# Attention: which engine forms the last half of each second head's low part

## The chip, the cores and the metric

The kernel is one program for one core of one Trainium2 chip. A core has engines that run side by side, each through its own instructions in their fixed order: TensorE (PE in the profile, its weight loads PEld), VectorE (DVE), ScalarE (ACT), GpSimd (POOL), and SyncE (SP), which here only starts DMA transfers. An instruction waits at the head of its engine's queue until what it needs is there, and all behind it on that engine wait with it. The metric is the time of one execution on the device in microseconds (us), the median of several runs. 1 us is 1000 ns.

## The reference, cut to what matters

Two layers, each an attention A and a gated MLP B, with a residual around each. The change lies in A, in the part where the softmax weights `p` meet the values.

```python
for s in range(N):                         # 4 segments of 512 rows, 32 heads of 20 columns
    qs, ks, vs = q[:, :, s], k[:, :, s], v[:, :, s]
    logits = jnp.einsum("bhqd,bhkd->bhqk", qs, ks) * scale + mask
    p = _softmax(logits, axis=-1)
    a_dot = jnp.einsum("bhqk,bhkd->bhqd", p, vs)
...
x = x + _A_ref(_layernorm(x, axis=-1), A_wq, A_wk, A_wv, A_wo, A_beta)
x = x + _B_ref(_layernorm(x, axis=-1), B_w_in, B_w_sp, B_b_sp, B_w_out)
x = x + _A_ref(_layernorm(x, axis=-1), A_wq, A_wk, A_wv, A_wo, A_beta)
x = x + _B_ref(_layernorm(x, axis=-1), B_w_in, B_w_sp, B_b_sp, B_w_out)
```

The products run on fp16 operands. So that little precision is lost, each fp32 operand is split in two fp16 parts: the high part is its rounding, the low part is what the rounding left over. For the softmax weights these are `PH` (high) and `PL = P - PH` (low), and both are multiplied with the values.

## The kernel before, in words

A layer's attention (`phase1a`) treats the 32 heads two at a time, in each of the four segments: 64 pairs of heads per layer, numbered `n`. Time is cut into steps `t` in `run`; five steps are a round, and a round carries two pairs, 2d and 2d+1, through the same stations. The order of the PE's instructions is that of the code (`manual_schedule` for PE alone); on the other engines a scheduler fixes the order when the program is built, within the limits that `issue_after` sets: `behind(DVE)` puts what is traced inside it behind the row maxima of the same step, `behind(ACT)` behind the exponentials of the same step.

In each step PE does, in this order: the logits by queries (`by_queries`, tile `mp` in PSUM, one buffer), from which DVE takes the row maxima (L935 and L938, `mxs`); the logits by keys (`by_keys`, tile `es`, one buffer), from which ACT forms the exponentials `P` (L913); the products of `PH` and `PL` with the values for the heads whose turn it is (`pvs`, L977, into `pv`); and then a share of the dense products (L677, L709, L736), which are spread over the steps. Since `mp` has one buffer, PE's logits of the next step wait for the row maxima of this one. DVE also finishes each pair (`combine`: `rs`, its reciprocal, `ab`, lines L988, L989, L993), splits the dense products, and does the layernorm statistics.

`cast` makes the two parts of a pair's head `h`: ACT copies `P` to `PH` (L947, 1280 columns), and then two instructions of 640 columns each form `PL` (L949). Before the change both run on GpSimd, but for head 1 of the layer's last two pairs (`TAIL`), where they run on DVE. In a round the heads are cast at steps 2, 3, 4 and 5 (that is step 0 of the next round): (2d, head 0), (2d, head 1), (2d+1, head 0), (2d+1, head 1). PE uses them at steps 5, 6, 8 and 8. `PL` has two buffers, so the low part of one head can be formed only after PE has read that of the head two before it. GpSimd also adds the two halves of each finished pair (L996, L997) and splits the finished heads (L1006).

Of the kernel before, what the change touches and what calls it, by code (L numbers as in the profile page):

```python
# [14 lines left out]
ALU = mybir.AluOpType  # L15
# [555 lines left out]
DVE, ACT = mybir.EngineType.DVE, mybir.EngineType.Activation  # L571


class Attention:
# [366 lines left out]
    def cast(self, n, h):  # L941

        nc = self.nc
        P = self.pair(n)
        PH = self.pl3.tile([128, 1280], F16, tag="PH", name="PH")
        PL = self.pl2.tile([128, 1280], F16, tag="PL", name="PL")
        nc.scalar.copy(PH, P[:, h])  # L947
        for c in (slice(0, 640), slice(640, 1280))[::-1 if n % 2 and h else 1]:
            (nc.gpsimd if h == 0 or n < self.N - self.TAIL else nc.vector).tensor_tensor(PL[:, c], P[:, h, c], PH[:, c], ALU.subtract)  # L949
        self.P[n, h] = (PH, PL)  # L950

    def maxes(self, d):
# [287 lines left out]
```

## Time and profile before

| | |
|---|---|
| median of 3 runs | 2309.6 us (2309.24 to 2312.05) |
| span of the profiled execution | 2318.3 us |
| first layer's rounds (from the first to the last L935) | 80.6 us to about 570 us |
| second layer's rounds | 1227 us to 1698 us |
| the remainder | the MLP of each layer, PE busy all along |

The profile's span is that of one execution, 8.7 us above the median of the runs; the runs themselves differ by 3 us. In the page, a row of the busy table gives an engine's busy time, its share of the span and its number of instructions. A row of the view by stretches gives the same per stretch of the span: the stretch, its length, then busy time and count of each engine. A row of the view of waits gives engine, line and tile that waited, for whom, the sum, how many times, and the longest. A row of the timeline gives start, duration, engine, line, operation, shapes and count; in brackets, the idle time of the engine ahead of it.

### The profile page before, as it was taken

What the parts mean: (1) busy time and instruction counts of PE and PEld (TensorE: products, weight loads), DVE (VectorE), ACT (ScalarE), POOL (GpSimd) and SP (SyncE); (2) the same over time, 40 slices, a digit from 0 to 9 for tenths busy, and PEclk for the clock granted to TensorE, in tenths of its full rate; (3) what the DMA queues carried; (4) which work ended last, traced back from release to release, by engine and by line L of the source; (5) the groups of instructions that cost most, each with busy time, mean ns of one, the idle gap of its engine ahead of it and who ended that gap; (6) DMA issues with size and microseconds to landing.
All of it is one profiled execution on the core that took longest, in us unless ns stands there. A gap on an engine that the chain in (4) does not pass through costs nothing.

```text
span 2318.3 us, 52548 instructions
## 1 busy us (share of the span) xinstructions
PE 2174.6 (94%) x21706; PEld 1309.5 (56%) x21706; DVE 1377.8 (59%) x2577; ACT 1139.2 (49%) x1344; POOL 991.4 (43%) x976
## 2 busy tenths in 40 slices
PE   5888898999899999999998989999989999999998
PEld 3455555666555555555555556566665555555554
DVE  7687888777755444444427786777766444534331
ACT  3587788888522222121125987888863222212110
POOL 2287889999611000000104988899991100000000
PEclk9999999999899999999999999999999999999999
DMA  5565665345743687565633465443565357766561
GB/s 166 145 164 150 168 172 132 89 113 142 207 119 96 153 219 168 149 168 148 147 96 97 111 157 129 120 109 107 128 177 124 99 119 202 158 160 160 157 147 46
DMA packets 504912, 325.59 MB, mean 140 GB/s; under 512 B 410688, under 2 KB 445632, under 8 KB 499552
## 3 DMA queue, kind: packets, MB, share of 16 engines
q1 hardware_dynamic: 504672, 322.23, 54.5%
q8 instruction: 170, 2.79, 0.5%
q14 instruction: 70, 0.57, 0.1%
HBM read 148.46 MB, written 85.61 MB: 101 GB/s over the span
## 4 chain that ended last, share of the span: by engine, by line
PE 66%; DVE 9%; DMA 8%; POOL 6%; ACT 6%; issue 3%; SPq 1%; DVEq 0%; ACTq 0%; POOLq 0%
PE gp L430 23%; PE zp L343 13%; PE cyp L459 8%; POOL PL L949 5%; PE pv L977 3%; PE qps L736 3%; PE kps L736 3%; PE vps L677 3%; PE mp L875 3%; DVE mxs L938 2%; PE yps L709 2%; PE es L875 2%; ACT P L913 1%; ACT PH L947 1%; DMA th<-xnhl 1%
## 5 line engine op out<-in xcount | busy, mean ns | idle before, releaser
L949 POOL TENSOR_TENSOR PL<-P,PH 128x640 f16<-128x640 f32 x380 | 538.8, 1444 | 53.2 <-PE pv L977 45.6
L430 PE MATMUL gp<-zh,wt 128*128 128x432 f16 x2048 | 462.2, 346 | 0.0
L430 PEld LDWEIGHTS <-wt 128*128 128x128 f16 x3072 | 300.5, 98 | 257.6
L938 DVE TENSOR_REDUCE mxs<-mp 128x2 f32<-128x1024 f32 (+2 forms) x384 | 320.4, 862 | 148.1 <-PE mp L866 146.5
L913 ACT ACTIVATE P<-es,sc 128x1024 f32<-128x1024 f32 (+1 forms) x256 | 271.6, 1061 | 100.0 <-PE es L866 89.5
L445 POOL MEMSET un<- 128x64 f16 x32 | 4.9, 152 | 665.3 <-DMA ut<-un 628.3
L343 PEld LDWEIGHTS <-th 128*128 128x128 f16 x1920 | 187.3, 98 | 169.4 <-DMA th<-xnhl 8.8
L430 PE MATMUL gp<-zl,wt 128*128 128x432 f16 x1024 | 270.5, 346 | 0.0
L433 ACT ACTIVATE u<-gp,bsp,un 128x864 f32<-128x864 f32 x32 | 34.3, 1071 | 431.2 <-PE gp L430 431.2
L252 POOL TENSOR_TENSOR lnrs<-lnve,mhalf 128x1 f32<-128x1 f32 x96 | 60.8, 641 | 429.1 <-DVE lnve L251 377.5
L947 ACT CAST PH<-P 128x1280 f16<-128x1280 f32 x192 | 239.7, 1248 | 1.5
L407 DVE TENSOR_REDUCE am<-wr 128x1 f32<-128x2048 f32 x32 | 73.2, 2286 | 220.0 <-DMA wr<-in_B_w_sp_dram 220.0
L677 PE MATMUL vps<-wvh,xt 128*128 128x320 f16 x640 | 158.5, 316 | 25.6 <-DVE relu L768 19.4
L949 POOL TENSOR_TENSOR PL<-Pb,PH 128x640 f16<-128x640 f32 x124 | 178.0, 1462 | 9.2 <-PE pv L977 9.2
L459 PE MATMUL cyp<-wuh,ut 128*128 128x320 f16 (+1 forms) x896 | 165.1, 301 | 5.7 <-DMA ut<-un 5.7
L875 PEld LDWEIGHTS <-qk 64*128 64x128 f16 (+1 forms) x2048 | 78.0, 94 | 163.0 <-issue 140.3
L459 PEld LDWEIGHTS <-ut 128*128 128x128 f16 (+1 forms) x1344 | 132.1, 98 | 61.5 <-DMA ut<-un 6.4
L977 PE MATMUL pv<-vs,PL 128*128 128x41 f16 x2560 | 157.6, 181 | 8.4 <-POOL PL L949 6.9
L977 PE MATMUL pv<-vs,PH 128*128 128x41 f16 x2560 | 160.0, 182 | 1.2 <-DVE ab L993 1.2
L875 PE MATMUL es<-qk 64*128 64x512 f16 (+3 forms) x1024 | 126.3, 303 | 31.7 <-ACT P L913 27.1
L343 PE MATMUL zp<-wi1h,th 128*128 128x432 f16 x640 | 147.8, 346 | 6.8 <-DMA th<-xnhl 6.8
L343 PE MATMUL zp<-wi0h,th 128*128 128x432 f16 x640 | 148.1, 346 | 0.0
(189 smaller groups left out, 4315.8 us busy)
## 6 DMA issues: line engine op xcount, KB each, us to landing
wr<-in_B_w_sp_dram SPq DMA_DIRECT2D x32, 1024.0 KB
qk<-st SPq DMA_DIRECT2D x256, 120.0 KB
z<-z SPq DMA_DIRECT2D x32, 432.0 KB
cz<-z SPq DMA_DIRECT2D x32, 432.0 KB
xt<-in_A_x_dram SPq DMA_DIRECT2D x32, 320.0 KB
st<-qhl SPq DMA_DIRECT2D x40, 256.0 KB
st<-khl SPq DMA_DIRECT2D x40, 256.0 KB
x<-x SPq DMA_DIRECT2D x32, 320.0 KB
```

The costliest lines, as they stand in the source:

```text
L343: nc.tensor.matmul(zp[:, n, :FHH], a[:, k, :], b[:, k, c:c + FHH], start=(k == 0 and j == 0), stop=(k == KD - 1 and j == 2))
L407: nc.vector.tensor_reduce(am, wr, AX.X, ALU.max, apply_absolute_value=True)
L430: nc.tensor.matmul(gp[:, n, :FHH], wt[:, k // 8, a, k % 8, :], b[:, k, n * FHH:(n + 1) * FHH], start=(k == 0 and j == 0), stop=(k == NT - ...
L459: nc.tensor.matmul(yp[:, n, :320], a[:kn[k], k, :], b[:kn[k], k, n * 320:(n + 1) * 320], start=(k == 0 and j == 0), stop=(k == KO - 1 and ...
L677: nc.tensor.matmul(ps, a[:, k, c], b[:, k, n * 320:(n + 1) * 320], start=(i == 0), stop=(i == 14))
L736: nc.tensor.matmul(ps, a[:, k, c], b[:, k, :], start=(i == 0), stop=(i == 14))
L875: nc.tensor.matmul(out[:, h, o:o + w], a[r, ac], b[r, bc], start=o == 0, stop=False, skip_group_check=True)
L913: self.lead.append(nc.scalar.activation(P, E, AF.Exp, scale=g.esc))
L938: e = nc.vector.tensor_reduce(mx[:, :, n, j], mp[:, :, o:o + w], AX.X, ALU.max)
L947: nc.scalar.copy(PH, P[:, h])
L949: (nc.gpsimd if h == 0 or n < self.N - self.TAIL else nc.vector).tensor_tensor(PL[:, c], P[:, h, c], PH[:, c], ALU.subtract)
L977: nc.tensor.matmul(pv[:, i, h, :], x[:, c:c + 128], v[:, j, h0 + h, :], start=(j == 0 and x is PH), stop=(j == i and x is PL), skip_group_ ...
```

## The change

The halves of head 1's low part are told apart: the second of the two goes to DVE in all pairs, not only the last two, and what goes to DVE is put behind the row maxima of its step. The first half of head 1, and both halves of head 0, stay on GpSimd. In the layer's last two pairs both halves of head 1 stay on DVE, now also behind the row maxima.

```diff
-        for c in (slice(0, 640), slice(640, 1280))[::-1 if n % 2 and h else 1]:
-            (nc.gpsimd if h == 0 or n < self.N - self.TAIL else nc.vector).tensor_tensor(PL[:, c], P[:, h, c], PH[:, c], ALU.subtract)
+        for i, c in enumerate((slice(0, 640), slice(640, 1280))[::-1 if n % 2 and h else 1]):
+            if h and (i or n >= self.N - self.TAIL):
+                with self.behind(DVE):
+                    nc.vector.tensor_tensor(PL[:, c], P[:, h, c], PH[:, c], ALU.subtract)
+            else:
+                nc.gpsimd.tensor_tensor(PL[:, c], P[:, h, c], PH[:, c], ALU.subtract)
```

62 instructions of each layer move, 124 in all: GpSimd keeps 380 of its 504 on this line, DVE has 132 in place of 8. The line numbers behind it grow by four (L949 becomes L951 on DVE and L953 on GpSimd, L988 becomes L992, and so on). PE's instructions stand as before, in every row. On ACT, SP and DVE the scheduler also exchanges some neighbours.

First place: DVE in the first layer's round at 493 us to 498 us of the profile of before, behind the two row maxima of the round's step 1 (the row with x2) up to the next maxima. Before:

```order
L938 TENSOR_REDUCE mxs_289<-mp 128x2 x2
L715 SCALAR_TENSOR_TENSOR xt<-yps,sc,xt 128x320
L988 TENSOR_TENSOR rs<-pv,iomg 128x8
L989 RECIPROCAL rs<-rs 128x8
L993 TENSOR_TENSOR ab<-pv,rs 128x328
L938 TENSOR_REDUCE mxs_288<-mp 128x2
```

and now:

```order
L938 TENSOR_REDUCE mxs_289<-mp 128x2 x2
L715 SCALAR_TENSOR_TENSOR xt<-yps,sc,xt 128x320
L951 TENSOR_TENSOR PL<-Pb,PH 128x640
L992 TENSOR_TENSOR rs<-pv,iomg 128x8
L993 RECIPROCAL rs<-rs 128x8
L997 TENSOR_TENSOR ab<-pv,rs 128x328
L938 TENSOR_REDUCE mxs_288<-mp 128x2
```

The half low part of pair 2d+1 now stands ahead of a finished pair's three instructions and of the next row maxima.

Second place: DVE a little later in the same round, behind the two row maxima of step 3 up to the four maxima of step 4 (L935). Before:

```order
L938 TENSOR_REDUCE mxs_288<-mp 128x2 x2
L715 SCALAR_TENSOR_TENSOR xt<-yps,sc,xt 128x320
L988 TENSOR_TENSOR rs<-pv,iomg 128x8
L989 RECIPROCAL rs<-rs 128x8
L993 TENSOR_TENSOR ab<-pv,rs 128x328
L935 TENSOR_REDUCE mxs_288<-mp 128x2x2
```

and now:

```order
L938 TENSOR_REDUCE mxs_288<-mp 128x2 x2
L715 SCALAR_TENSOR_TENSOR xt<-yps,sc,xt 128x320
L992 TENSOR_TENSOR rs<-pv,iomg 128x8
L993 RECIPROCAL rs<-rs 128x8
L997 TENSOR_TENSOR ab<-pv,rs 128x328
L951 TENSOR_TENSOR PL<-P,PH 128x640
L935 TENSOR_REDUCE mxs_288<-mp 128x2x2
```

The half low part of pair 2d, head 1, stands directly ahead of L935. In some rounds it stands directly behind it.

Third place: GpSimd in that round. Before:

```order
L949 TENSOR_TENSOR PL<-P,PH 128x640 x2
L996 TENSOR_TENSOR ab<-ab,gm 128x8x20
L949 TENSOR_TENSOR PL<-P,PH 128x640 x2
L997 TENSOR_TENSOR gm<-ab 128x4x40
L949 TENSOR_TENSOR PL<-Pb,PH 128x640 x4
L996 TENSOR_TENSOR ab<-ab,gm 128x8x20
L997 TENSOR_TENSOR gm<-ab 128x4x40
```

and now:

```order
L953 TENSOR_TENSOR PL<-P,PH 128x640 x2
L1000 TENSOR_TENSOR ab<-ab,gm 128x8x20
L953 TENSOR_TENSOR PL<-P,PH 128x640
L1001 TENSOR_TENSOR gm<-ab 128x4x40
L953 TENSOR_TENSOR PL<-Pb,PH 128x640 x3
L1000 TENSOR_TENSOR ab<-ab,gm 128x8x20
L1001 TENSOR_TENSOR gm<-ab 128x4x40
```

Six halves stand in the round where there were eight.

## The prediction, as put on record before the changed kernel ran

> **What bounds the kernel now.** I read the page first, then busy time by stretches, then who waits for the line that is changed, and last the timeline of one round.
>
> ```profile
> span 2318.3 us, 52548 instructions
> PE 2174.6 (94%) x21706; PEld 1309.5 (56%) x21706; DVE 1377.8 (59%) x2577; ACT 1139.2 (49%) x1344; POOL 991.4 (43%) x976
> 80.00:400.00 320.00, 280.26 (x4127) 173.51 (x4123) 261.94 (x476) 255.88 (x321) 253.67 (x223) 0.96 0.59 154
> 400.00:600.00 200.00, 187.65 (x3002) 126.03 (x2994) 147.55 (x275) 163.88 (x185) 193.28 (x179) 0.97 0.49 129
> 1240.00:1540.00 300.00, 275.68 (x4173) 174.35 (x4173) 230.18 (x420) 252.37 (x312) 260.35 (x234) 0.98 0.50 126
> 1540.00:1690.00 150.00, 145.32 (x2377) 96.30 (x2377) 107.97 (x201) 124.85 (x143) 144.70 (x139) 1.00 0.44 113
> ```
>
> The page's shares say little: they mix two attentions with two MLPs, where GpSimd rests. The four stretches are the attentions; their columns are stretch, length, PE, PEld, DVE, ACT, POOL. In the second and fourth GpSimd is busy for 193.28 of 200 us and 144.70 of 150, 96.6% and 96.5%: it sets the pace, and PE, with 12.35 and 4.68 us not busy, runs beside it with little room. In the first and third no engine is full (GpSimd 79% and 87%, DVE 82% and 77%, PE 88% and 92%); PE there is without work for 39.7 and 24.3 us.
>
> ```profile
> L949 POOL TENSOR_TENSOR PL<-P,PH x380: 1389/1403/2215, 101.4 to 1728.7; 128x640 f16<-128x640 f32 x190
> L949 DVE TENSOR_TENSOR PL<-P,PH x4: 843/1414/2018, 604.9 to 1731.2; 128x640 f16<-128x640 f32 x4
>   PEld L977: 9.6, 11
>   ACT P L913: 9.2, 10
>   PE pv L977: 8.4, 11
> DVE mxs L938 <- PE mp L866: 30.1, 25, 4.1
> DVE mxs L935 <- PE mp L866: 4.8, 8, 1.0
> ```
>
> The first two rows are the line that moves, on either engine: count, then shortest, middle and longest in ns. The three after it are all who waited for it in the whole span: 9.6, 9.2 and 8.4 us. PE's two rows are largely the same waits seen at the loads and at the matmuls. The last two are from the waits between 400 and 560 us: even where GpSimd sets the pace DVE is idle only in pieces, mostly ahead of row maxima that wait for PE's logits.
>
> **What the change takes and adds.** The two engines disturb each other on this instruction:
>
> ```profile
> 605.06 1.98 POOL L949 TENSOR_TENSOR PL<-P,PH 128x640 f16<-128x640 f32 x1
> 605.70 2.02 DVE L949 TENSOR_TENSOR PL<-P,PH 128x640 f16<-128x640 f32 x1
> ```
>
> The GpSimd instruction began at 605.06 and ended at 607.04; DVE's, begun at 605.70, ended 0.68 us after that, at 607.72. Its 2.02 us are thus 1.34 of standing still and 0.68 of work. GpSimd's 1.98 are the ordinary 1.40 plus 0.58 for the DVE instruction before it. So a moved half takes 1.40 us off GpSimd and gives back 0.58: 0.82 net, 124 x 0.82 = 102 us, 1.64 us per round. On DVE it costs 0.68 plus what is left of GpSimd's instruction at that moment. Bounds: 0.68 (GpSimd idle) and 2.02 (the row above). I take 1.38: with the new positions set into the timeline of before, the remainder at the 118 places that a later row of maxima follows is 0.70 on average, close to the middle value of the four rows, 1.414. In all DVE gets 124 x 1.38 = 171 us.
>
> The Trainium skill, SBUF — State Buffer, section Who interferes with whom, says that a DVE instruction with two SBUF inputs contends with a GpSimd instruction that reads SBUF, and that the second to issue blocks until the first ends. By that rule, the two rows agree: each stood still while the other worked, and neither ran at half rate.
>
> Set into the stretches (34, 25, 36 and 21 moved halves), DVE's busy time at an unchanged length becomes 261.94 + 46.9 = 308.8 of 320 us (96.5%), 182.1 of 200 (91%), 279.9 of 300 (93%) and 137.0 of 150 (91%). That looks like room, but DVE's work comes in a fixed order, and PE's next logits wait for each row of maxima. What matters is where the half stands. One round, with both places (the order rows of the change show them):
>
> ```profile
> 492.15 1.25 ACT L947 CAST PH<-Pb 128x1280 f16<-128x1280 f32 x1
> 492.48 5.48 POOL L949 TENSOR_TENSOR PL<-Pb,PH 128x640 f16<-128x640 f32 x4
> 494.56 0.54 DVE L715 SCALAR_TENSOR_TENSOR xt<-yps,sc,xt 128x320 f32<-128x320 f32 x1
> 495.02 0.16 DVE L988 TENSOR_TENSOR rs<-pv,iomg 128x8 f32<-128x8 f32 x1
> 495.93 1.22 DVE L938 TENSOR_REDUCE mxs<-mp 128x2 f32<-128x1024 f32 x1
> 498.04 0.39 PE L875 MATMUL mp<-qk 60*128 60x384 f16 x4
> 499.59 2.77 POOL L949 TENSOR_TENSOR PL<-P,PH 128x640 f16<-128x640 f32 x2 [0.61 <-PE pv L977]
> 499.88 1.25 ACT L947 CAST PH<-P 128x1280 f16<-128x1280 f32 x1
> 500.76 0.50 DVE L993 TENSOR_TENSOR ab<-pv,rs 128x328 f32<-128x328 f32 x1
> 501.74 1.23 DVE L935 TENSOR_REDUCE mxs<-mp 128x4 f32<-128x1024 f32 x1 [0.49 <-PE mp L866]
> 503.37 0.39 PE L875 MATMUL mp<-qk 60*128 60x512 f16 x2
> ```
>
> First place, behind L715, which ends at 495.10. `PH` has been there since 493.40; GpSimd's second half of four (1.37 apart) ends at 495.22. The new half ends about 495.9; `rs` and all behind it start 0.9 later, the maxima of 495.93 end about 498.1, and PE wants the logits' buffer at 498.04: no delay to speak of. With the mean of 1.38 it would be 0.6. Second place, behind `ab`, which ends at 501.26. `PH` came at 501.13; GpSimd's second half of two began about 500.97 and has 1.1 left, so the new half takes 1.78 and ends at 503.04. DVE had been idle for 0.49 there. L935 then ends at 504.27 rather than 502.97, and PE, which started the next logits at 503.37, starts 0.9 later.
>
> ```profile
> L935 DVE TENSOR_REDUCE mxs<-mp x64: 1214/1226/1228, 80.6 to 1698.2; 128x4 f32<-128x1024 f32 x64
> ```
>
> The same working at all 118 places, in the rounds between the first and last of these rows, gives delays between 0 and 2.3 us, 0.66 on average: **78 us gross** (26.4, 13.2, 25.6 and 11.8 by stretch, 0.9 behind them). Each was worked out by itself, so a wait that PE has anyway later in the round takes part of it back. That part is the open term. In the first and third stretch (52 us gross) PE's idle 39.7 + 24.3 = 64 us could absorb all of it or, since much of that time is spent on this very chain, little: 0 to 52 us stay. I take 21, nearer to the lower end, because PE's own idle is the larger number. GpSimd's relief in these two is part of its 8.4 to 9.6 us of waits; I take 7 off. In the second and fourth stretch (25 us gross) the relief can return at most PE's 12.35 + 4.68 = 17.0 us; I take all of it: 25 - 17 = +8. **Sum: 21 - 7 + 8 = +22 us**, between -24 (no delay stays, all relief comes) and +77 (all stays, no relief).
>
> Another look at the first term: the same twelve rounds in both layers.
>
> ```profile
> 103.20:316.00 212.80, 183.46 (x2740) 114.22 (x2737) 175.11 (x321) 173.32 (x218) 174.05 (x149) 0.94 0.60 158
> 1249.80:1444.00 194.20, 177.02 (x2735) 111.76 (x2731) 145.45 (x264) 163.61 (x203) 169.35 (x149) 0.97 0.50 128
> ```
>
> The first layer's have 29.7 us more DVE work (the scales and splits of the weights), some more ACT work and transfers, and are 18.6 us longer, 0.63 us per us of DVE. The first and third stretch get 70 x 1.38 = 97 us; at that rate it would be 61. Since ACT, the transfers and the clock (0.94 against 0.97) differ too, this is an upper end, and it agrees with 52 rather than 0.
>
> What else is added costs nothing by itself: no DMA moves to another engine, PE's order is unchanged, and the eight halves of the last pairs were on DVE already. The new wait is DVE's on ACT's `PH`: behind it stand `rs`, `ab` and the maxima. In the round above it was there 1.7 and 0.1 us earlier; where ACT is late, that delay is in the 78 us.
>
> **The rivals.** (1) *Faster*: DVE's half disappears in idle time. The place is that ahead of L935 and of the next single maxima; the price is the 17.0 us of the second and fourth stretch gained, less 6 in the others: -11, 2298.6 us. It decides if the half takes 0.9 us or less on average, which is 0.2 of blocking: possible, since GpSimd has a quarter fewer such instructions. For it speaks that GpSimd is at 96.6%; against it the middle value of 1.414, though from eight rows only. (2) *No change*: the exchange is level, 2309.6 us: all the relief that can reach PE, 7 + 17 = 24 us, comes, and 24 of the 78 us stay. The Trainium skill, Perfetto Trace Analysis, section Optimizing Scalar/DVE Operations, says that moving work between these two might not help because they share a read port of SBUF. By that rule alone the sum would be 0; the trace agrees only in part, since GpSimd keeps 0.82 of each 1.40. (3) *DVE becomes the bound*: the first stretch at 96.5% in a fixed order cannot hold its length, all 52 us stay with the 7 us of relief, and the others come out level: 2309.6 + 45 = 2354.6. For it, 82% is DVE's highest share in any stretch so far; against it, PE's idle of 64 us. (4) That the change would not do what it says is excluded: the order rows show 124 instructions on DVE.
>
> **How the numbers follow.** The sum is a difference and was made in the profiled execution of 2318.3 us span; it is added to the median, 8.7 us below it: 2309.6 + 22 = **2331.6**. Chances: forecast 0.48, rival 3 and worse 0.12, level 0.13, faster 0.27. Its own range is 2316 to 2356 (from little left in the first and third stretch to all of it). The range for 8 in 10 reaches to rival 1 and rival 3: 2298 to 2356. 0.2% of this kernel is 4.6 us, about what a measurement can tell from none; the chances are 0.27 faster, 0.13 same, 0.60 slower.
>
> **What would show it.** L951 on DVE at 1.2 to 1.5 us on average, with 0.68 as its least, and GpSimd's L953 still 1.40 in the middle with more of them near 1.98. GpSimd's share in the second stretch falls from 96.6% to near 85%, DVE's rises over 90%. PE's waits for the `mxs` rows grow, its waits for `PL` go. I am wrong in the blocking if the DVE half is 0.9 or less; wrong in the absorption if it is 1.4 and the first stretch is no longer; wrong in the relief if the second and fourth stretch, with GpSimd at 85%, are shorter by over 17 us.

## The result, and the profile after

| | before | changed |
|---|---|---|
| median, 4 runs each | 2310.82 us (2309.24 to 2312.55) | 2365.63 us (2364.72 to 2369.32) |
| ratio | | 1.0242, 95% interval 1.0228 to 1.0256 |

The change costs 54.8 us. The sign is the forecast's, the size is two and a half times the +22, and it lies outside the range. First the changed kernel's span and busy table, then the moved line by tile (shortest, middle, longest in ns):

```profile
span 2364.6 us, 52612 instructions
PE 2177.3 (92%) x21706; PEld 1314.9 (56%) x21706; DVE 1523.4 (64%) x2701; ACT 1142.6 (48%) x1344; POOL 861.4 (36%) x852
```

```profile
L951 DVE TENSOR_TENSOR PL<-P,PH x98: 769/1637/2052, 103.3 to 1776.9; 128x640 f16<-128x640 f32 x98
L951 DVE TENSOR_TENSOR PL<-Pb,PH x34: 801/1220/2010, 128.1 to 1781.3; 128x640 f16<-128x640 f32 x34
L953 POOL TENSOR_TENSOR PL<-P,PH x286: 1387/1402/2212, 100.4 to 1773.0; 128x640 f16<-128x640 f32 x143
```

DVE gained 145.6 us of busy time, GpSimd lost 130.0. GpSimd's ordinary half is still 1.40 us; DVE's takes anything from 0.77 to 2.05. By group, DVE's two kinds:

```profile
L951 DVE TENSOR_TENSOR PL<-P,PH 128x640 f16<-128x640 f32 x98 | 143.2, 1462 | 7.1 <-ACT PH L947 6.8
L951 DVE TENSOR_TENSOR PL<-Pb,PH 128x640 f16<-128x640 f32 x34 | 42.4, 1251 | 0.0
```

(143.2 + 42.4) / 132 = 1.406 us on average. The records of the halves sum to 174 us more than before (185.6 against 11.5); DVE's busy time rose by less, because the records of neighbours overlap (by 0.08 us at 462.82 in the timeline below) and because some other DVE instructions got shorter (L774 by 4.8 us in all).

Since PE's order is unchanged, a layer's rounds can be cut at the starts of the same L935 in each kernel: the 3rd, the 22nd and the last of the layer's 32. "Early" is then nineteen rounds, "late" the last ten. The view by stretches (length, then busy time and count of PE, PEld, DVE, ACT, POOL, then PE's granted clock, the share of the DMA engines and GB/s), for the kernel before, early and late of each layer:

```profile
103.16:431.64 328.48, 289.91 (x4386) 184.80 (x4384) 266.41 (x492) 269.08 (x336) 280.66 (x250) 0.96 0.59 152
431.64:569.93 138.29, 134.61 (x2211) 88.23 (x2209) 101.85 (x188) 116.33 (x133) 133.13 (x127) 1.00 0.43 114
1249.84:1559.88 310.04, 284.97 (x4383) 183.12 (x4381) 235.65 (x435) 259.05 (x321) 275.58 (x250) 0.98 0.49 124
1559.88:1698.18 138.30, 134.63 (x2211) 88.21 (x2209) 101.86 (x189) 116.34 (x133) 133.15 (x127) 1.00 0.45 119
```

and the same four of the changed kernel:

```profile
102.15:455.64 353.49, 297.02 (x4398) 189.81 (x4395) 311.07 (x531) 270.87 (x337) 238.52 (x213) 0.95 0.54 141
455.64:599.01 143.37, 133.96 (x2197) 88.60 (x2197) 126.97 (x209) 116.15 (x132) 115.17 (x106) 1.00 0.41 110
1277.32:1602.01 324.69, 286.39 (x4395) 185.36 (x4392) 279.54 (x475) 261.09 (x322) 237.13 (x213) 0.98 0.46 119
1602.01:1745.64 143.63, 133.96 (x2197) 88.62 (x2197) 127.21 (x208) 116.16 (x132) 115.15 (x106) 1.00 0.43 115
```

The counts of PE show that the cuts fall 12 to 14 matmuls apart in the two kernels, under 1 us. The early rounds grew by 25.0 and 14.7 us, the late by 5.1 and 5.3: +50.1 in all. (The spans differ by 46.3 and the medians by 54.8: the profiled execution of the kernel before took some 9 us longer than its median, so differences against it read a little low.) In the late rounds GpSimd went from 96.3% to 80% and DVE from 74% to 89%, yet they are longer.

Who makes PE wait now, from the view of waits (sum in us, times, longest), changed kernel:

```profile
PE mp L875 <- DVE mxs L938: 24.6, 34, 1.3
PE mup L829 <- DVE mr L964: 19.6, 10, 2.8
PE mp L875 <- DVE mxs L935: 14.9, 21, 1.7
PE pv L981 <- DVE ab L997: 11.3, 10, 2.8
POOL ab L1000 <- DVE ab L997: 63.7, 34, 3.2
POOL gm L1001 <- DVE ab L997: 43.3, 13, 8.7
```

and the same of the kernel before:

```profile
PE mup L829 <- DVE mr L960: 8.2, 7, 2.0
PE mp L875 <- DVE mxs L938: 5.8, 14, 1.1
PE mp L875 <- DVE mxs L935: 3.6, 6, 1.6
PE pv L977 <- DVE ab L993: 1.2, 3, 0.8
POOL gm L997 <- DVE ab L993: 6.9, 5, 4.2
```

Three things of DVE hold PE up: the row maxima, 9.4 us before and 39.5 after; `mr`, 8.2 and 19.6; and `ab`, 1.2 and 11.3. Together that is 51.6 us more. (`mr` is what DVE forms from the transposed row maxima; PE's products `mup` need the PSUM buffer that it reads. `ab` frees PE's one buffer of finished products.) GpSimd, which was to be relieved, now stands for 107 us behind DVE's `ab`, against 10.7 before (6.9 in the row above and 3.8 for its own `ab`).

One place of the first kind, some rounds ahead of the one shown with the change, in the changed kernel's timeline (start, duration; cut to the rows that matter):

```profile
461.11 1.10 POOL L1010 TENSOR_TENSOR ohl<-gm,ohl 128x480 f16<-128x480 f32 x1
461.45 1.45 DVE L951 TENSOR_TENSOR PL<-Pb,PH 128x640 f16<-128x640 f32 x1
462.17 1.99 POOL L953 TENSOR_TENSOR PL<-Pb,PH 128x640 f16<-128x640 f32 x1
462.82 0.15 DVE L992 TENSOR_TENSOR rs<-pv,iomg 128x8 f32<-128x8 f32 x1
463.13 1.17 DVE L938 TENSOR_REDUCE mxs<-mp 128x2 f32<-128x1024 f32 x1
464.21 0.49 DVE L997 TENSOR_TENSOR ab<-pv,rs 128x328 f32<-128x328 f32 x1
464.38 0.39 PE L875 MATMUL mp<-qk 60*128 60x384 f16 x4
464.78 0.50 POOL L1000 TENSOR_TENSOR ab<-ab,gm 128x160 f32<-128x160 f32 x1 [0.63 <-DVE ab L997]
```

DVE's half stands until GpSimd's instruction ends at 462.21 and works until 462.90 (0.69 us). `rs`, the maxima and `ab` follow in a row; the maxima end at 464.30 and PE's next logits start at 464.38. GpSimd's half begun at 462.17 is stretched to 1.99 us, and its next instruction still waits 0.63 us for `ab`. PE's products ahead of these logits ran until 464.44 by the profile, so this place holds up GpSimd and costs PE hardly anything; elsewhere PE does wait for L938, up to 1.3 us at a time (first row of the view of waits).

The chain that ended last, before and after (page):

```profile
PE 66%; DVE 9%; DMA 8%; POOL 6%; ACT 6%; issue 3%; SPq 1%; DVEq 0%; ACTq 0%; POOLq 0%
```

```profile
PE 62%; DVE 20%; DMA 6%; ACT 4%; issue 4%; POOL 2%; SPq 1%; DVEq 0%; ACTq 0%; POOLq 0%
```

DVE's share has more than doubled, and GpSimd's fell from 6% to 2%: it was never much of the chain.

### The profile page after: what moved, and what is told of

Read it like the earlier page. It is cut to its first block, busy times and chain, and to the rows that moved or that the text cites. A ratio compares the mean times of both kernels' runs of the same rounds, so it can differ in the third digit from the quotient of the medians.

```text
span 2364.6 us, 52612 instructions
## 1 busy us (share of the span) xinstructions
PE 2177.3 (92%) x21706; PEld 1314.9 (56%) x21706; DVE 1523.4 (64%) x2701; ACT 1142.6 (48%) x1344; POOL 861.4 (36%) x852
## 4 chain that ended last, share of the span: by engine, by line
PE 62%; DVE 20%; DMA 6%; ACT 4%; issue 4%; POOL 2%; SPq 1%; DVEq 0%; ACTq 0%; POOLq 0%
PE gp L430 22%; PE zp L343 13%; PE cyp L459 8%; DVE mxs L938 5%; DVE PL L951 4%; PE vps L677 3%; PE pv L981 3%; PE mp L875 2%; PE qps L736 2%; PE kps L736 2%; PE yps L709 2%; DVE mxs L935 2%; DMA th<-xnhl 1%; ACT PH L947 1%; PE es L875 1%
## 5 line engine op out<-in xcount | busy, mean ns | idle before, releaser
L953 POOL TENSOR_TENSOR PL<-P,PH 128x640 f16<-128x640 f32 x286 | 418.9, 1483 | 91.8 <-PE pv L981 83.6
L938 DVE TENSOR_REDUCE mxs<-mp 128x2 f32<-128x1024 f32 (+2 forms) x384 | 319.5, 859 | 95.5 <-PE mp L866 94.2
L981 PE MATMUL pv<-vs,PH 128*128 128x41 f16 x2560 | 160.4, 183 | 11.6 <-DVE ab L997 11.3
L875 PE MATMUL mp<-qk 60*128 60x512 f16 (+3 forms) x1024 | 128.0, 307 | 42.1 <-DVE mxs L938 24.6
L981 PEld LDWEIGHTS <-PL 128*128 128x128 f16 x2560 | 142.0, 97 | 14.9 <-issue 10.4
```

The lines of the kernel that those rows point to most:

```text
L875: nc.tensor.matmul(out[:, h, o:o + w], a[r, ac], b[r, bc], start=o == 0, stop=False, skip_group_check=True)
L938: e = nc.vector.tensor_reduce(mx[:, :, n, j], mp[:, :, o:o + w], AX.X, ALU.max)
L953: nc.gpsimd.tensor_tensor(PL[:, c], P[:, h, c], PH[:, c], ALU.subtract)
L981: nc.tensor.matmul(pv[:, i, h, :], x[:, c:c + 128], v[:, j, h0 + h, :], start=(j == 0 and x is PH), stop=(j == i and x is PL), skip_group_ ...
```

## The experiments

Differences in us are those of the medians, or of the ratio where that is said, each against the kernel before run beside it on the same chip (2308.5 to 2311.5 us). The diffs are cut to the lines that matter; `...` stands for the rest. Theory 1 says that the half costs by the time it takes up on DVE, standing or working, ahead of things PE waits for; theory 2 that only the work counts; theory 3 that the new order and its waits do it, whatever the half lasts.

**e1: the relief alone.** The 124 halves are formed by nobody, and PE reads `PH` in their place.

```diff
-            if h and (i or n >= self.N - self.TAIL):
+            if h and n >= self.N - self.TAIL:
                 ...
-            else:
+            elif not (h and i):
                 nc.gpsimd.tensor_tensor(...)
 ...
+                    nc.tensor.matmul(pv[:, i, h, :], (PH if out else x)[:, c:c + 128], ...)
```

> Leaves out the moved halves: in all pairs but the last two of a layer the last half of head 1's low part is formed by nobody, and PE multiplies the high part in its place, so that PE does the same work. GpSimd is relieved of 1.40 us per half, DVE gets nothing. This prices the relief alone, put at 24 us at most in the prediction. If the relief can reach PE: 2281 to 2300 us. If PE has no use for it (the loss of the change is then all cost and no lost gain): 2305 to 2312 us.

Measured: 2298.11 us (2294.92 to 2300.04), ratio 0.9945 [0.9926, 0.9963]: -12.7 us by the ratio, -11.8 by the medians. Its four stretches:

```profile
101.30:421.34 320.04, 287.49 (x4386) 184.60 (x4384) 264.20 (x493) 268.65 (x336) 227.31 (x212) 0.97 0.59 156
421.34:558.54 137.20, 134.37 (x2213) 88.08 (x2211) 101.47 (x188) 115.92 (x132) 107.34 (x107) 1.00 0.43 115
1235.51:1541.69 306.18, 282.24 (x4383) 181.50 (x4381) 234.52 (x436) 258.93 (x321) 224.03 (x212) 0.99 0.50 126
1541.69:1678.90 137.21, 134.39 (x2214) 88.09 (x2212) 101.48 (x189) 115.93 (x133) 107.35 (x107) 1.00 0.44 119
```

GpSimd falls from 96.3% to 78% of the late rounds, and they get 1.1 us shorter in each layer. PE had 134.6 us of work in 138.3, so there was little more to gain. This kernel is also the yardstick for the cost: it has the relief and not the DVE half, so the changed kernel minus this one is what the half costs on DVE. That is 33.5 + 18.5 = 52.0 us early and 6.2 + 6.4 = 12.6 late. (The profiled execution of e1 was its fastest, 3.2 us below its median, so these may read a few us high.)

**e2: the same DVE place, no blocking.** DVE fills the half from one SBUF input (a reduction over one element; `PH` is not subtracted).

```diff
+            if h and i and n < self.N - self.TAIL:
+                with self.behind(DVE):
+                    nc.vector.tensor_reduce(PL[:, c], P[:, h, c].unsqueeze(2), AX.X, ALU.max)
 ...
```

> The moved half is formed on DVE by an instruction that reads one SBUF tensor (a maximum over one element of P; the high part is not subtracted), at the same place behind the row maxima. Expected on DVE: about 0.7 us each with no standing still, and no GpSimd instruction longer than 1.41 because of it. Theory 1 (all time that DVE spends at that place counts, working or standing, because the row maxima behind it come later): half of the time is left, with the full relief, 2300 to 2330 us. Theory 2 (only DVE's work counts, its standing still falls into time that it had anyway): 2340 to 2365. Theory 3 (the new order and the added edges, not the time): 2350 to 2366.

**e5: standing without work.** DVE forms only the last 8 of the 640 columns, GpSimd the other 632.

```diff
 ...
+            if h and i:
+                e = slice(c.stop - 8, c.stop)
+                c = slice(c.start, c.stop - 8)
+                with self.behind(DVE):
+                    nc.vector.tensor_tensor(PL[:, e], P[:, h, e], PH[:, e], ALU.subtract)
             nc.gpsimd.tensor_tensor(PL[:, c], P[:, h, c], PH[:, c], ALU.subtract)
```

> DVE forms only the last 8 columns of each moved half, at the same place, and GpSimd the other 632: the same order, the same wait for the high part and for GpSimd's port, almost no work and no relief. Expected on DVE: 0.1 us of work and up to 1.4 of standing still. Theory 1 (standing counts like working): 2335 to 2355 us. Theory 2 (only the work counts): 2311 to 2318. Theory 3 (order and edges): 2350 to 2366.

Measured: e2 2321.66 us (2316.72 to 2327.53), 1.0053 [1.0035, 1.0072], +12; e5 2339.57 us (2333.89 to 2342.53), 1.0119 [1.0088, 1.0151], +27 by the ratio. A row of e2 (the other 30 have the same middle value):

```profile
L951 DVE TENSOR_REDUCE PL<-P x94: 797/808/822, 98.1 to 1721.8; 128x640 f16<-128x640 f32 x94
```

and of e5:

```profile
L957 DVE TENSOR_TENSOR PL<-P,PH x94: 156/837/1408, 102.2 to 1744.1; 128x8 f16<-128x8 f32 x94
L957 DVE TENSOR_TENSOR PL<-Pb,PH x30: 146/666/1409, 126.3 to 1727.2; 128x8 f16<-128x8 f32 x30
```

In e2 the half never stands: 0.80 to 0.82 us. In e5 the instruction works for about 0.15 us, its shortest, and lasts up to 1.41, one whole GpSimd half. The two take almost the same DVE time, 124 x 0.81 = 100 us of work in e2 and 98 us (94 x 0.811 + 30 x 0.720, the groups' means) in e5, of which only 124 x 0.15 = 19 are work and the rest is standing. (As DVE's busy time it is 74 us more than in e1 and 85 more than in the kernel before.) e2 costs 12 + 12.7 = some 24 us over the relief alone; e5, with hardly any relief (GpSimd busy for 987.0 us against 991.4), costs 27. Standing still costs like working: theory 2 falls. Theory 3 falls as well: with the half at the same place e2 costs 43 us less than the changed kernel. One thing more differs in e2: its half doesn't wait for `PH`. For that wait DVE was idle 6.8 us ahead of the changed kernel's halves, and 11.2 in e5; the runs don't price it by itself.

**e3 and e4: one place each.** Only the even, or only the odd pairs' halves move (62 each).

```diff
-            if h and (i or n >= self.N - self.TAIL):
+            if h and (i and n % 2 == 0 or n >= self.N - self.TAIL):     # e3; n % 2 == 1 in e4
```

> Only the even pairs' halves move (62 of 124), those that stand directly ahead of or behind L935. If both places cost alike: 2335 to 2343 us. If the place ahead of L935 is the dear one: over 2345. If the odd pairs' place, ahead of a pair's three closing instructions and the next maxima, is the dear one: under 2325. The gross delays worked out from the timeline of before were 33 us for the even places and 45 for the odd ones.

> Only the odd pairs' halves move (62 of 124), those that stand ahead of a pair's three closing instructions and the next single maxima. The even ones alone had cost 13 us, the whole change 55. If the two places add up: 2348 to 2355 us. If the loss grows faster than the time on DVE, because delays of one place no longer run out before the next: 2320 to 2340.

Measured: e3 2323.43 us (2320.45 to 2330.23), 1.0058 [1.0036, 1.008], +13; e4 2355.37 us (2348.56 to 2360.03), 1.0197 [1.0175, 1.0219], +46. The sum, 59, is near the 55 of the whole, so the places roughly add up (e4 lies 0.4 us above the range named for that). The moved half lasts about the same in both (means of 1.44 us in e3, 1.41 and 1.33 in e4). Who makes PE wait in e3:

```profile
PE mp L875 <- DVE mxs L935: 17.7, 23, 1.7
PE mup L829 <- DVE mr L964: 10.1, 8, 2.0
PE mp L875 <- DVE mxs L938: 7.4, 17, 0.8
PE pv L981 <- DVE ab L997: 7.0, 4, 2.4
```

and in e4:

```profile
PE mp L875 <- DVE mxs L938: 24.4, 35, 1.2
PE mup L829 <- DVE mr L964: 19.2, 9, 3.1
PE pv L981 <- DVE ab L997: 11.3, 9, 2.8
PE mp L875 <- DVE mxs L935: 4.2, 9, 1.1
```

The even half delays mainly the four maxima behind it (L935). The odd half stands ahead of `rs` and `ab`, of the next maxima (L938) and of `mr`, and delays all of them. The gross delays of the forecast had been 33 for the even and 45 for the odd places; they were far less alike.

**e7: the late rounds alone** (pairs from 38 on).

```diff
+            if h and (i and n >= 38 or n >= self.N - self.TAIL):
```

> The halves move only in pairs from 38 on, the part of each layer where GpSimd was 96% busy before and DVE least (rounds 21 to 30 took 5 us more per layer in the changed kernel's profile). If the late rounds' loss is their own: 2318 to 2324 us, and the other 45 us belong to the early rounds. If it is carried over from the early rounds, and the relief works once they are left alone: 2303 to 2311.

Measured: 2322.71 us (2321.58 to 2324.11), 1.0058 [1.0043, 1.0073], +13. In the rounds where GpSimd was 96% busy the exchange loses by itself; it isn't something left over from the early rounds.

**e8: the even half one step later,** on DVE behind L935 instead of ahead of it (odd halves stay on GpSimd).

```diff
 ...
+            elif h and i and n % 2 == 0:
+                self.post(1, lambda c=c: nc.vector.tensor_tensor(PL[:, c], P[:, h, c], PH[:, c], ALU.subtract))
```

> Only the even pairs' halves move, as in the run of the even pairs (13 us slower than before), but one step later: behind the four maxima (L935), ahead of the next single maxima. If it is L935's lateness that costs: 2306 to 2314 us. If a half ahead of any row maxima costs the same: 2319 to 2327.

Measured: 2329.51 us (2328.74 to 2331.73), 1.009 [1.0074, 1.0107], +20, where e3 has +13. A miss of both ranges: PE's wait for L935 falls to 4.2 us, but that for L938 rises to 13.3. The half now holds up the next maxima in line; this place isn't free either.

**e9: the odd half two steps later,** behind `rs`, `ab` and the single maxima; even halves stay on GpSimd. **e10: the odd half where the change put it, from one input** as in e2.

```diff
 ...
+            elif h and i and n % 2:      # e9
+                self.post(2, lambda c=c: nc.vector.tensor_tensor(PL[:, c], P[:, h, c], PH[:, c], ALU.subtract))
```

> Only the odd pairs' halves move, as in the run of the odd pairs (46 us slower than before), but two steps later: behind the pair's three closing instructions (rs, reciprocal, ab) and the single maxima that they had stood ahead of, in front of the next two maxima. Same work, same blocking. Theory 1a (the dear thing is what stands directly behind the half: the closing instructions, which free PE's one buffer of finished products, and the maxima and mr behind them): 2315 to 2335 us, and PE's waits for ab (11 us there) and for mr (19 us) fall to about those of before (1 and 8). Theory 1b (any time on DVE at any place costs alike, by load): 2345 to 2358.

> Only the odd pairs' halves move, at the changed kernel's place, but formed from one SBUF input, so that neither engine stands still for the other: 0.81 us each on DVE in place of 1.37, and the high part is not subtracted. All halves in this manner had cost 12 us, all with two inputs 55. If the loss goes with the time on DVE (0.81 of 1.37, and 6 us more relief): 2325 to 2335 us. If nearly all of it is the standing still: 2305 to 2318. If it is the place alone, whatever the time: 2345 to 2356.

Measured: e9 2334.16 us (2328.66 to 2336.89), 1.0107 [1.0086, 1.0129], +25.6; e10 2330.34 us (2327.43 to 2333.6), 1.0099 [1.0081, 1.0117], +21.8; against +46 in e4. Who makes PE wait in e9:

```profile
PE mup L829 <- DVE mr L966: 21.5, 10, 3.2
PE mp L875 <- DVE mxs L938: 6.9, 16, 1.1
PE mp L875 <- DVE mxs L935: 3.6, 5, 1.3
PE pv L983 <- DVE ab L999: 3.3, 4, 1.5
```

Compared with e4 the maxima went from 28.6 to 10.5 us and `ab` from 11.3 to 3.3; `mr`, which still comes behind the half, did not fall as had been expected. So the waits follow the place. But the place is not the whole gain: two steps later the half lasts 0.99 us on average instead of 1.33 to 1.41, so it stands less. e10 shows that a shorter half at the old place gains about as much (there GpSimd is also relieved of 17 us more). In e10 PE waits 14.5 us for the maxima and 15.2 for `mr`, less than in e4, but 11.4 for `ab`, just as in e4: the wait for `ab` goes with the place, that for the maxima with the place and the length. Both causes act on the odd half; the runs don't split e9's 20 us between them.

**e11: all 124 halves moved, the odd ones two steps later.**

```diff
 ...
+            if h and i and n % 2 and n < self.N - self.TAIL:
+                self.post(2, lambda c=c: nc.vector.tensor_tensor(PL[:, c], P[:, h, c], PH[:, c], ALU.subtract))
+            elif h and (i or n >= self.N - self.TAIL):
 ...
```

> All 124 halves on DVE as in the change, the even pairs' at the changed kernel's place, the odd pairs' two steps later, behind rs, ab and the single row maxima. If the two places add up, as 13 and 46 did for the change, this is 13 + 26 = 39 us above the kernel before: 2343 to 2353. If DVE's total load decides and the place does not, it is as slow as the change, 2358 to 2368. If the two moved halves come to stand close together and disturb each other, above 2368.

Measured: 2344.87 us (2343.59 to 2347.26), 1.0141 [1.0119, 1.0163], +33. With the same 124 instructions on DVE as in the change, a later place takes off 21 us. DVE's busy time falls with it, from 1523.4 to 1492.1 us, since the odd halves stand less (middle 0.82 us). It is still slower than leaving the halves on GpSimd.

**e6: shorter GpSimd instructions.** The changed kernel, GpSimd's halves cut in two pieces of 320 columns. **e12: the same cut in the kernel before,** nothing moved. The diff shown is that of e6.

```diff
+                for c in (slice(c.start, c.start + 320), slice(c.start + 320, c.stop)):
                     nc.gpsimd.tensor_tensor(PL[:, c], P[:, h, c], PH[:, c], ALU.subtract)
```

> The changed kernel, but GpSimd forms its halves in two pieces of 320 columns each, so that DVE never waits for more than about 0.75 us for it. Same work on DVE, a little more on GpSimd (one instruction more per half). Expected on DVE: 1.05 us on average in place of 1.41. Theory 1 (standing still counts like working): 2335 to 2352 us. Theory 2 (only the work counts): 2362 to 2372, GpSimd's added starts included.

> Nothing moved: the kernel before with GpSimd's halves cut in two pieces of 320 columns. Theory that the pieces helped the changed kernel only because DVE stands shorter behind a shorter GpSimd instruction: here they bring nothing, 2305 to 2314 (a price for more instructions on GpSimd, busy for 96.5% of the late rounds, would show as up to 2325). Rival, that shorter pieces speed up GpSimd or hand PL to PE earlier: under 2303, and then the gain of 21 us seen on the changed kernel is not the blocking's alone.

Measured: e6 2344.79 us (2343.39 to 2355.4), 1.0163 [1.014, 1.0187], +35; e12 2349.97 us (2337.72 to 2350.69), 1.0152 [1.0127, 1.0177], +35 by the ratio. In e6 the DVE half falls to 1.15 and 1.14 us on average, and the loss against the kernel before is 19 us smaller than the change's. e12 missed all its ranges: the cut alone makes the kernel before slower by as much as moving the halves costs in e6, so under the cut the move costs nothing that these runs can tell (there it also spares GpSimd the dearer pieces). How much of these 19 us is the shorter block and how much that, the two runs don't say. A GpSimd piece takes 0.795 us, two of them 0.19 more than one whole, 8 x 0.19 = 1.5 us per round. The late rounds of e12 (the first layer's; the second's are 145.06 us long):

```profile
440.32:585.37 145.05, 136.09 (x2209) 88.77 (x2206) 102.34 (x189) 115.37 (x132) 143.29 (x204) 1.00 0.38 109
```

They are 6.8 us longer than before, with GpSimd 98.8% busy. So GpSimd sets the pace once it has more to do; with 2.6 us less per round (133.1 against 107.3 in ten, e1) it is PE that does. The rounds before lie just where the two meet.

No kernel that does the whole computation was faster than the kernel before.

## Why the prediction was right in sign and too small

| step of the forecast | put at | shown |
|---|---|---|
| a half on DVE | 1.38 us | 1.406 us |
| taken off GpSimd, net | 0.82 per half, 102 us | 1.05 per half, 130 us |
| relief, early rounds | 7 | at most 12.3 (before minus e1) |
| relief, late rounds | 17 | 2.2 (before minus e1) |
| delays that stay, early | 21 of 52, row maxima alone | 52.0 (changed minus e1), 15.9 of it row maxima |
| delays that stay, late | 25 of 25 | 12.6 (changed minus e1) |
| sum | +22 | +50.1 in the rounds |

The early relief is an upper end: over the whole kernel e1 gains 12.7 us by the ratio, and the 9 us by which the profiled execution of the kernel before is too long may lie in its early rounds.

**Right:** the size of the half and its blocking (its shortest is 0.77 us, where 0.68 had been said). By the rule cited from the Trainium skill (SBUF — State Buffer, Who interferes with whom) the second to issue blocks; the 8-column instruction that lasts up to 1.41 us agrees, and so do the 0.80 to 0.82 us of the instruction with one input. Right too is where the wait appears (row maxima), that GpSimd's share falls (80% of the late rounds; near 85% had been said), and that the waits for `PL` mostly go: PE's idle time ahead of these matmuls, 8.4 us before, is 3.2 after. DVE does not go over 90%: 86 to 89%, since the rounds got longer.

**The step that failed is the term of the delays that stay in the early rounds:** "0 to 52 us stay. I take 21, nearer to the lower end, because PE's own idle is the larger number." The 52 were delays of the row maxima, the only victim that the working priced; the finished pair's `ab` and `mr`, which stand behind the half too, were put at nothing without a reason, and so was PE's own work. 52.0 us came, but they are mostly not those 52. Who makes PE wait in e1, which has the relief and not the DVE half:

```profile
PE mup L829 <- DVE mr L964: 11.5, 8, 2.0
PE mp L875 <- DVE mxs L935: 4.3, 8, 1.6
PE mp L875 <- DVE mxs L938: 3.5, 9, 0.6
PE pv L982 <- DVE ab L998: 1.4, 2, 0.8
```

Against these 7.8 us for the row maxima the changed kernel has 39.5: 32 of the 78 us gross, less than the 46 that the forecast let stay. The same view, taken by stretches, gives for the early rounds, changed kernel against e1:

| early rounds, both layers | e1 | changed | more |
|---|---|---|---|
| waits for the row maxima | 5.2 | 21.1 | 15.9 |
| waits for `ab` | 0.8 | 10.0 | 9.2 |
| waits for `mr` | 11.4 | 19.6 | 8.2 |
| PE busy | 569.7 | 583.4 | 13.7 |
| length | 626.2 | 678.2 | 52.0 |

The remaining 5 us are smaller waits, up and down. So the priced victim cost less than the 21, and the terms left out cost 31. That the sum equals the whole gross delay is chance. Where the other 36 us of it went, into PE's idle time or because the working was too high, no run tells. PE's idle time as a whole was no reserve: it grew from 56.5 us in e1's early rounds to 94.8.

PE's longer busy time isn't waiting. Under 2 us of it are 24 matmuls more between the cuts; for the rest the rows show a granted clock of 0.95 and 0.98 against 0.97 and 0.99 in e1. This is not peculiar to the profiled execution: all four of the changed kernel have a mean clock of 0.980 or 0.981, the five of e1 0.984 to 0.987, and the twelve of the kernel before run beside e1 0.982 to 0.988. Whether PE's pauses bring the clock down or something else does, no run here tells.

**The relief in the late rounds was mis-sized as well.** The forecast took 17.0 us of idle PE from stretches that do not end with the rounds. Of the 12.35 us in the second stretch 7.2 lie in the 30 us behind the last round, and 1.4 ahead of the late rounds. Cut at the rounds, PE has 3.7 us idle per layer, and e1 returns 1.1 of them. "It sets the pace" was read from 96.6%; GpSimd was one of two engines at the limit, PE at 97.3% being the other. The late delays came out at half of the 25: PE's waits for the row maxima grew by 15.7 us and those for ACT fell by 2.7. By luck the two errors nearly cancel: +8 forecast, +10.4 measured.

**The rivals.** (1) asked for halves of 0.9 us or less. Even at 0.81 us (e2) the kernel is slower by 12, so its price was wrong as well as its condition. (2) fell: the exchange is not level. By the rule cited for it from the Trainium skill (Perfetto Trace Analysis, Optimizing Scalar/DVE Operations) the move might not help; here it hurts, by 2.4%. (3) came nearest: all 52 us early, and +45 in all, still 10 below the result. Its reason, DVE at its limit there, is not what is seen: DVE is at 88% and 86%, and the 52 agree by chance as above. What counts is the place in the queue and how long the half holds it (e4 against e3, e9, e10).

## What to carry to other kernels

When an instruction is inserted into an in-order queue, list everything behind it that another engine waits for, not only the nearest, and price each (here the two victims left out cost PE 17 us of waits in the early rounds, the one that was priced 16). Don't take idle time of the waiting engine for a reserve unless a run shows that it takes the delay up. Before moving work off a nearly full engine, leave that work out once (as e1 does): here that showed 12.7 us to win in all, less than the half costs on DVE in any of the variants tried. And cut the stretches at the loop's own events, since the 30 us of a layer's end held 7.2 of the 12.35 us for which PE looked idle beside a full GpSimd.

## What the runs showed of the hardware that was not expected

- A DVE instruction of 8 columns with two SBUF inputs lasts up to 1.41 us beside a GpSimd instruction, nine times its 0.15. The profile counts that as busy time, so a busy share on DVE hides standing.
- DVE gives back less to GpSimd than the one pair of rows of before suggested: of 124 x 1.40 = 174 us, 130.0 left GpSimd, so at most 0.35 us per half came back, not 0.58.
- Cutting a GpSimd subtraction of 640 columns in two costs 0.19 us of GpSimd (2 x 0.795 against 1.40), and in a kernel at the limit that alone made the whole 1.5% slower.
